# Attention, FFT mixing and FFN on one core: the FFN of batches 1 to 7 in one block of 512 tokens each and a last block of the left-over 448, with TensorE in program order there

## The chip, the cores and the metric

The program runs on one NeuronCore of a Trainium2 chip. A core has a matmul engine (TensorE, PE in the profile), VectorE (DVE), ScalarE (ACT), GpSimd (POOL) and SyncE (SP), which issues most DMAs here. The metric is the device time of one execution in microseconds; the median of three runs before the change is 1087.92 us (1087.62 to 1090.3).

## The reference

Eight batches of 576 tokens. The first half is attention over 8 heads with keys and values averaged over groups of 8 tokens; its result x (576 x 512 per batch) goes through a two-dimensional FFT of which the real part is kept, a residual, a normalization and a feed-forward network (FFN) of width 2048:

```python
attn = softmax(scale * q @ pool8(k).T) @ pool8(v)      # 8 x 8 heads x 576 x 64
x = attn, heads side by side                           # 8 x 576 x 512
X = np.fft.fft(np.fft.fft(x, axis=1), axis=2)
u = x + np.real(X)
mu = np.mean(u, axis=-1, keepdims=True)
var = np.mean((u - mu) ** 2, axis=-1, keepdims=True)
un = (u - mu) / np.sqrt(var + 1e-06)
ch = np.maximum(un @ w_ch1, 0.0) @ w_ch2
return u + ch
```

## The kernel before

Channels lie on the 128 partitions in four tiles (E0, O0, E1, O1), tokens along the free dimension. Each fp32 operand of the two large products is held as a high and a low part, so a product takes three matmul passes: high by high, high by low, low by high.

The **front end** of a batch, `fe(b)`, is a generator that works in steps: loads and averages keys and values, scores (psS, L345), softmax, transposition (psT, psR), attention times values (psX, L432, two halves of 288 tokens per group of heads), then the FFT as cosine and sine matmuls over sums of mirrored positions. The sum of the even channels is `tmpE` (L510), its parts are `f` (L503 on ScalarE, L504 on VectorE), and psA (L547), psB (L575), psQ and psP (L592) are the products. Then come the mean (psM, L638 to L643), the centred values in two parts `unh` and `unl`, the squares (`qh`, and `ql` L664), the variance (psVar, L667) and three Newton steps for the inverse root `rb`. All matmuls of the front ends use rotating PSUM banks that a function `bank` gives out.

The **FFN**, `ffn` (L705), works through the hidden width in 16 slices f of 128. For each f it issues 12 matmuls into g1 (L731), the relu `hh` on ScalarE (L735), its low part `hl` on VectorE (L736), and 12 matmuls into four accumulators acc0 to acc3 (L715) for the slice before. It yields after each such group of 12 matmuls; this is a half step. After the last slice VectorE multiplies the accumulators by `rb` (L745), adds U (L746), and SP sends the result out (L748). The low parts of the weights are kept in DRAM and read back for every f of every block, 256 KB for each of the two products (`load_low`, L214, in a ring of seven buffers with the tag "w"); the high parts stay on chip.

Unnormalized sums U, `unh`, `unl` and `rb` have a ring of two batches, 1152 columns. `blocks()` (L71) lists the blocks of the FFN: batch 0 in two halves of 288 tokens, each in two parts of 8 slices; batches 1 to 6 as nine blocks of 384 tokens over the ring, so a block may lie across two batches; batch 7 as two blocks of 288. That makes 208 slice steps.

The order of the instructions on each engine is fixed when the program is built, by a scheduler that plays the program through with its own durations: on TensorE it may take front-end matmuls and FFN matmuls in another order than the code has them. The code sets when a front-end step is issued: `advance(pos)` (L790) runs one step of each front end per half step, from positions in `free` (L753).

Of the kernel before, what the change touches and what calls it, by code (L numbers as in the profile page):

```python
# [83 lines left out]
def tile_kernel(ctx: ExitStack, tc: tile.TileContext, qt, kt, vm, vr, w1, w2, cad, cbd, mkd, out):  # L84
# [93 lines left out]
    def prep_w(n):  # L178
# [4 lines left out]
        if wide:  # L183
# [61 lines left out]


    def fe(b):
# [82 lines left out]
        def scores(gi, i):  # L330
# [374 lines left out]
    def ffn(ro, nb, to, f0, f1):  # L705
        cl = slice(ro, ro + nb)
        acc = [pp.tile([P, 512], F32, tag=f"acc{e}", name=f"acc{to}_{f0}_{e}")[:, 0:nb] for e in range(4)]
# [224 lines left out]
```

## Time and profile before

| | before |
|---|---|
| median of 3 runs | 1087.92 us |
| the profiled execution: time, span | 1088.63 us, 1086.9 us |
| TensorE busy | 1044.1 us, 96% |
| VectorE, ScalarE, GpSimd busy | 609.4, 415.0, 249.4 us |
| from the first matmul of 384 columns to the last matmul's start | 244.5 to 1080.1 us |

Busy time of an engine counts its computing instructions; a matmul is pipelined, so its listed duration is longer than the time by which the next one follows. The time from one matmul to the next is read from the starts in the timeline.

### The profile page before, as it was taken

To read this page: it belongs to the slowest core of one execution; us is meant where nothing else is said; L and a number is where in the kernel's file an instruction comes from. 1 tells how busy PE (TensorE), PEld (TensorE's weight loads), DVE (VectorE), ACT (ScalarE), POOL (GpSimd) and SP (SyncE) were. 2 spreads that over 40 slices of the span, in tenths; PEclk is the share of its full clock that TensorE was granted. 3 is DMA by queue.
4 is the path that set the end of the run, shared out by engine and by line. 5 is a ranking of instruction groups with operands and counts; after the bars stand their busy time and mean duration, and the time that the engine had idled before them with its cause. 6 is when DMAs were issued, how large, how long until landed. Compare 5 with 4: busy or idle time off the path is not lost.

```text
span 1086.9 us, 17702 instructions
## 1 busy us (share of the span) xinstructions
PE 1044.1 (96%) x6606; PEld 1018.9 (94%) x6606; DVE 609.4 (56%) x1237; ACT 415.0 (38%) x1102; POOL 249.4 (23%) x249
## 2 busy tenths in 40 slices
PE   8848898999999999999999999999999999999997
PEld 7737788999999999999999999999999999999997
DVE  7686878856376455756277455656467434522212
ACT  6767764543143341443233341443324422311110
POOL 4464355312240032201240122300331101300000
PEclk9878998999999999999999999999999999999999
DMA  7767976675445454445444454445435334446563
GB/s 246 259 215 249 330 253 213 191 201 165 127 122 162 123 167 133 128 141 162 139 122 147 140 155 132 135 125 156 158 108 157 97 107 123 115 131 185 166 187 99
DMA packets 91878, 175.80 MB, mean 162 GB/s; under 512 B 10128, under 2 KB 17296, under 8 KB 91536
## 3 DMA queue, kind: packets, MB, share of 16 engines
q1 hardware_dynamic: 91504, 172.01, 51.7%
q0 software_dynamic: 288, 2.66, 0.6%
q8 instruction: 52, 0.85, 0.3%
q14 instruction: 34, 0.28, 0.1%
HBM read 156.81 MB, written 17.83 MB: 161 GB/s over the span
## 4 chain that ended last, share of the span: by engine, by line
PE 85%; DVE 5%; DMA 4%; ACT 2%; POOL 2%; issue 1%; SPq 0%; DVEq 0%; POOLq 0%; ACTq 0%
PE acc L715 35%; PE g L731 35%; PE psX L432 3%; PE psS L345 3%; PE psP L592 2%; DMA k<-in_kt 1%; PE psA L547 1%; PE psB L575 1%; PE psT L385 1%; PE psQ L592 1%; DVE wd L199 1%; POOL k L280 1%; DMA w2l<-wd 1%; DVE wd L198 1%; PE psR L408 1%
## 5 line engine op out<-in xcount | busy, mean ns | idle before, releaser
L735 ACT ACTIVATE hh<-g 128x384 fp32r<-128x384 f32 (+1 forms) x208 | 96.2, 463 | 305.4 <-PE g L731 285.6
L736 DVE SCALAR_TENSOR_TENSOR hl<-g,hh 128x384 fp32r<-128x384 f32 (+1 forms) x208 | 108.6, 522 | 185.0 <-ACT hh L735 179.4
L715 PE MATMUL acc<-hh,w2h 128*128 128x384 f32 (+1 forms) x832 | 190.5, 329 | 0.2 <-DVE U L746 0.2
L715 PE MATMUL acc<-hh,w2low 128*128 128x384 f32 (+1 forms) x832 | 186.8, 327 | 0.3 <-DMA w2low<-w2l 0.3
L715 PE MATMUL acc<-hl,w2h 128*128 128x384 f32 (+1 forms) x832 | 182.3, 328 | 1.1 <-DVE hl L736 1.1
L731 PE MATMUL g<-unh,w1low 128*128 128x384 f32 (+1 forms) x832 | 178.2, 329 | 1.6 <-DMA w1low<-w1l 1.6
L731 PE MATMUL g<-unl,w1h 128*128 128x384 f32 (+1 forms) x832 | 177.8, 328 | 1.0 <-DVE unl L633 1.0
L731 PE MATMUL g<-unh,w1h 128*128 128x384 f32 (+1 forms) x832 | 175.6, 328 | 0.0
L715 PEld LDWEIGHTS acc<-hh,w2h 128*128 128x128 f32 x832 | 143.1, 189 | 2.6 <-ACT hh L735 0.7
L715 PEld LDWEIGHTS acc<-hh,w2low 128*128 128x128 f32 x832 | 144.0, 189 | 0.6 <-DMA w2low<-w2l 0.5
L715 PEld LDWEIGHTS acc<-hl,w2h 128*128 128x128 f32 x832 | 141.4, 190 | 2.1 <-DVE hl L736 1.7
L731 PEld LDWEIGHTS g<-unh,w1low 128*128 128x128 f32 x832 | 141.0, 190 | 2.0 <-DMA w1low<-w1l 1.8
L731 PEld LDWEIGHTS g<-unl,w1h 128*128 128x128 f32 x832 | 140.7, 190 | 1.4 <-DVE unl L633 1.3
L731 PEld LDWEIGHTS g<-unh,w1h 128*128 128x128 f32 x832 | 140.7, 191 | 1.3 <-issue 0.8
L364 POOL TENSOR_TENSOR t<-t,sm 128x720 f32<-128x720 f32 x32 | 47.0, 1469 | 284.6 <-DVE sm L363 247.3
L280 POOL TENSOR_TENSOR k<-k 128x288 f32<-128x288 f32 (+1 forms) x56 | 42.3, 755 | 97.1 <-DMA k<-in_kt 73.3
L624 POOL TENSOR_TENSOR U<-X,U 128x576 f32<-128x576 f32 (+1 forms) x14 | 20.0, 1433 | 124.9 <-DVE X L608 124.9
L345 PE MATMUL psS<-kpb,q 128*128 128x144 f32 x280 | 43.2, 289 | 3.8 <-DVE X L608 2.1
L345 PEld LDWEIGHTS psS<-kpb,q 128*128 128x128 f32 x280 | 39.8, 191 | 4.2 <-issue 2.3
L349 DVE TENSOR_REDUCE mx<-psS 128x6 f32<-128x432 f32 (+1 forms) x64 | 33.1, 525 | 18.9 <-PE psS L345 18.6
L360 ACT ACTIVATE t<-t 128x720 f32<-128x720 f32 x30 | 24.1, 804 | 37.3 <-DVE t L358 37.0
L745 DVE TENSOR_TENSOR acc<-acc,rb 128x384 f32<-128x384 f32 (+1 forms) x60 | 29.0, 518 | 13.8 <-PE acc L715 13.5
(209 smaller groups left out, 1425.7 us busy)
## 6 DMA issues: line engine op xcount, KB each, us to landing
w1low<-w1l SPq DMA_DIRECT2D x208, 256.0 KB, 2.7
w2low<-w2l SPq DMA_DIRECT2D x208, 256.0 KB, 2.9
wst<-in_w SPq DMA_DIRECT2D x30, 512.0 KB, 4.7
q<-in_qt SPq DMA_DIRECT2D x28, 288.0 KB, 3.1
k<-in_kt SPq DMA_DIRECT2D x28, 288.0 KB, 2.9
v<-in_vm SPq DMA_DIRECT2D x28, 256.0 KB, 3.0
out<-U SPq DMA_DIRECT2D x18, 384.0 KB, 3.5
w1l<-wd SPq DMA_DIRECT2D x16, 256.0 KB, 4.4
```

Of the source, the lines that this page charges most:

```text
L280: nc.gpsimd.tensor_tensor(out=out if n == 1 else src[:, :, 0:n], in0=src[:, :, 0] if n == 1 else src[:, :, 0:n], in1=src[:, :, 1] if n == ...
L345: mm = nc.tensor.matmul(ps[:, c * W2J:(c + 1) * W2J], lhsT=q[:, r0:r0 + P], rhs=kpb[g % 2], start=True, stop=True)
L349: nc.vector.tensor_reduce(out=mx[:, c0:c0 + n], in_=pv, op=ALU.max, axis=AX.X, negate=(b, g) in SM)
L360: nc.scalar.activation(t, t, AF.Exp, scale=1.0 / 64.0)
L364: ins = nc.gpsimd.tensor_tensor(out=t, in0=t, in1=sm.unsqueeze(3).broadcast_to([P, 5, 2, J]), op=ALU.mult)
L432: last = nc.tensor.matmul(ps, lhsT=w, rhs=a, start=(i == 0), stop=(i == len(mm) - 1))
L592: nc.tensor.matmul(ps, lhsT=w, rhs=a, start=(i == 0), stop=(i == 6))
L715: nc.tensor.matmul(acc[e], lhsT=w[:, e], rhs=h, start=(f == f0 and x == 0), stop=(f == f1 - 1 and x == 2))
L731: nc.tensor.matmul(ps, lhsT=w[:, c], rhs=x[:, ti, cl], start=(n == 0), stop=(n == 11))
L735: nc.scalar.activation(hh, ps, AF.Relu)
L736: nc.vector.scalar_tensor_tensor(out=hl, in0=ps, scalar=0.0, in1=raw(hh), op0=ALU.max, op1=ALU.subtract)
L745: nc.vector.tensor_tensor(out=acc[e], in0=acc[e], in1=rb[:, cl], op=ALU.mult)
```

## The change

Batch 0 keeps its four parts of 288 columns. Each batch from 1 to 7 has one block of its first 512 tokens. The last 64 tokens of each (U, `unh`, `unl`, `rb`) are written to DRAM by `keep_rest` when the batch's front end ends, four DMAs, and read back by `load_rest` in the block of batch 7 after its fifth half step, into the ring's free half; a last block of 448 columns computes these. There are 160 slice steps in place of 208. The program's host part puts the tokens back in order.

Within each block from batch 1 on, TensorE is under `manual_schedule`: its instructions keep the order in which the code issues them. Tables give the half step of a block after which each front-end step is issued: PRE (steps up to the FFT, for the batch two ahead) and POST (the steps from the FFT on, for the next batch); PRE1, POST1 and LATE are for the first two blocks. Front ends from batch 2 on follow a new generator, `steady`, which does the same matmuls, with 22 steps before and 10 behind; `tmpE` and `f` come at the end of its 22nd step. While batch 0's FFN runs, `early` issues steps of front end 2.

The "w" ring has six buffers in place of seven, `hh` and `hl` have 512 columns, the first two batches' diagonal `dg` has a tile and a PSUM bank of its own (before: X[:, 1] and psVar's bank), and from batch 2 on GpSimd does two of the four sums at a block's end.

```diff
+NB = 512
+FIRST = 64
+RM = S - NB
+PRE = [2, 4, 7, 8, 10, 12, 15, 16, 18, 18, 19, 20, 21, 22, 23, 24, 25, 26, 28, 29, 30, 31]
...
+POST = [4, 5, 6, 9, 10, 11, 14, 15, 16, 17]
...
-    r = [(slot(0) + h * HS, HS, h * HS, f, f + 8) for f in (0, 8) for h in range(2)]
-    for m in range(3):
-        r += [(i * 384, 384, S + m * RING + i * 384, 0, NFC) for i in range(3)]
-    return r + [(slot(7) + h * HS, HS, 7 * S + h * HS, 0, NFC) for h in range(2)]
+    r = [(0, slot(0) + h * HS, HS, h * HS, f, f + 8) for f in (0, 8) for h in range(2)]
+    r += [(b, slot(b), NB, S + (b - 1) * NB, 0, NFC) for b in range(1, B)]
+    return r + [(B, slot(0), (B - 1) * RM, S + (B - 1) * NB, 0, NFC)]
...
+    def keep_rest(b):
+        cl = slice(slot(b) + NB, slot(b) + S)
+        for t, r in zip((raw(unh), raw(unl), U), rests):
+            nc.sync.dma_start(r[:, :, b - 1], t[:, :, cl])
+        nc.sync.dma_start(rests[3][:, 0, b - 1], rb[:, cl])
...
-        lows[i, n] = t = wk.tile([P, DM], F32R, tag="w", bufs=7, name=f"w{i + 1}low")
+        lows[i, n] = t = wk.tile([P, DM], F32R, tag="w", bufs=6, name=f"w{i + 1}low")
...
-        dg = X[:, 1]
+        dg = wk.tile([P, S], F32, tag="k", name="dg")
...
+        ps = bank(b, f"psD{b}", True)
...
-            nc.vector.tensor_tensor(out=acc[e], in0=acc[e], in1=rb[:, cl], op=ALU.mult)
-            nc.vector.tensor_tensor(out=u, in0=u, in1=acc[e], op=ALU.add)
+            v = raw(gt(2 + e, "v"))[:, 0:nb] if e < 2 and b > 1 else acc[e]
+            nc.vector.tensor_tensor(out=v, in0=acc[e], in1=rb[:, cl], op=ALU.mult)
+            (nc.gpsimd if e < 2 and b > 1 else nc.vector).tensor_tensor(out=u, in0=u, in1=v, op=ALU.add)
...
+        advance(2, min(len(PRE1), n2 + (len(PRE) - n2) * (pos + 1) / FIRST))
...
     for blk in blocks():
-        for _ in ffn(*blk):
...
+        b = blk[0]
+        with tc.manual_schedule(engines={mybir.EngineType.PE}) if b else ExitStack():
+            for h, _ in enumerate(ffn(*blk)):
+                if b == 0:
+                    early()
+                    pos += 1
+                    continue
+                if b == B - 1 and h == 4:
+                    load_rest(slot(0))
+                if b in LATE:
+                    advance(b + 1, len(PRE1) + sum(x <= h for x in LATE[b]))
+                pre, post = (PRE1, POST1) if b == 1 else (PRE, POST)
+                advance(b + 1, len(PRE) + sum(x <= h for x in post) if h >= post[0] else 0)
+                advance(b + 2, sum(x <= h for x in pre))
```

**TensorE at the start of batch 3's psA.** Names: acc576 belongs to the block of batch 1, g1_1088 to that of batch 2 (acc960 and g1_960 to a block of 384 before); psA3_0 and psA3_1 are the two groups, f holds high and low part of `tmpE`. Before:

```order
L715 MATMUL acc960_0_2_4063<-hl_4434,w2h_69 128x384
L715 MATMUL acc960_0_3_4064<-hl_4434,w2h_69 128x384
L731 MATMUL g1_960_13_4486<-unh_83,w1h6_1993 128x384 x4
L731 MATMUL g1_960_13_4486<-unl_84,w1h6_1993 128x384 x2
L547 MATMUL psA3_0_3795<-ca_70,f_3759 128x258 x4
L547 MATMUL psA3_1_3805<-ca_70,f_3759 128x258 x4
L547 MATMUL psA3_0_3795<-ca_70,f_3760 128x258 x2
L547 MATMUL psA3_0_3795<-ca_70,xe_79 128x258
L547 MATMUL psA3_1_3805<-ca_70,f_3760 128x258 x2
L547 MATMUL psA3_1_3805<-ca_70,xe_79 128x258
```

After, from the last matmuls of block 1:

```order
L926 MATMUL acc576_0_3_2949<-hh_3927,w2h7_2288 128x512
L926 MATMUL acc576_0_3_2949<-hh_3927,w2low_3841 128x512
L926 MATMUL acc576_0_3_2949<-hl_3928,w2h7_2288 128x512
L942 MATMUL g1_1088_1_4045<-unh_87,w1low_4020 128x512
L358 MATMUL psA3_0_4067<-ca_74,f_3981 128x258 x4
L358 MATMUL psA3_0_4067<-ca_74,f_3982 128x258 x2
L358 MATMUL psA3_0_4067<-ca_74,xe_83 128x258
L358 MATMUL psA3_1_4077<-ca_74,f_3981 128x258 x4
L358 MATMUL psA3_1_4077<-ca_74,f_3982 128x258 x2
L358 MATMUL psA3_1_4077<-ca_74,xe_83 128x258
L926 MATMUL acc1088_0_0_4016<-hh_4037,w2h_73 128x512
```

Where psA's two groups stood side by side in the middle of an FFN block, with the matmuls on the high part of both ahead of those on the low part, each group now stands whole, one behind the other, at the change from one block to the next.

**VectorE between the last psX of batch 3 and the low part of tmpE.** Names: X is the attention's result, rb and U belong to block 1. Before:

```order
L445 TENSOR_TENSOR X_80<-psX3_1_3736,X_80 128x288
L510 TENSOR_TENSOR tmpE_3755<-X_80 128x2x287
L327 SCALAR_TENSOR_TENSOR rw1_78<-vt_4805,mk_72,rw1_78 32x1
L277 TENSOR_REDUCE vs_5111<-v4_0_4929 128x64
L277 TENSOR_REDUCE vt_5109<-vr4_1_4931 32x64
L504 TENSOR_TENSOR f_3760<-tmpE_3755,f_3759 128x580
```

After:

```order
L651 TENSOR_TENSOR X_84<-psX3_1_3964,X_84 128x288
L328 TENSOR_TENSOR tmpE_3971<-X_84 128x2x287
L957 TENSOR_TENSOR acc576_0_0_2946<-acc576_0_0_2946,rb_86 128x512
L520 SCALAR_TENSOR_TENSOR wlo_4441<-vs_4438,mk_76,wh_4440 128x1
L529 SCALAR_TENSOR_TENSOR rw1_82<-vt_4322,mk_76,rw1_82 32x63
L529 SCALAR_TENSOR_TENSOR rw1_82<-vt_4322,mk_76,rw1_82 32x1
L957 TENSOR_TENSOR acc576_0_1_2947<-acc576_0_1_2947,rb_86 128x512
L957 TENSOR_TENSOR acc576_0_2_2948<-acc576_0_2_2948,rb_86 128x512
L957 TENSOR_TENSOR acc576_0_3_2949<-acc576_0_3_2949,rb_86 128x512
L958 TENSOR_TENSOR U_85<-U_85,acc576_0_0_2946 128x512
L340 TENSOR_TENSOR f_3982<-tmpE_3971,f_3981 128x580
```

The four products with rb and a sum of block 1's end, 512 columns each, now stand between `tmpE` and its low part (L340, before L504).

## Rows read from the trace of the kernel before

**Rows 1.** The page's first two parts: TensorE's busy time with its share of the span and its instructions, then the busy tenths of TensorE and of VectorE in 40 slices of 27.2 us.

```profile
PE 1044.1 (96%) x6606; PEld 1018.9 (94%) x6606; DVE 609.4 (56%) x1237; ACT 415.0 (38%) x1102; POOL 249.4 (23%) x249
PE   8848898999999999999999999999999999999997
DVE  7686878856376455756277455656467434522212
```

**Rows 2.** Busy time of the engines by stretch: the stretch in us and its length, then for each engine the busy time with its instructions, the granted TensorE clock, the DMA share and GB/s.

```profile
150.00:200.00 50.00, 44.13 (x298) 41.35 (x297) 39.42 (x78) 26.73 (x64) 28.40 (x33) 0.93 0.72 226
200.00:250.00 50.00, 50.00 (x378) 49.54 (x377) 30.78 (x81) 21.28 (x60) 7.41 (x5) 1.00 0.62 183
250.00:600.00 350.00, 350.00 (x2150) 347.23 (x2149) 204.32 (x407) 123.82 (x331) 76.65 (x74) 1.00 0.47 142
600.00:960.00 360.00, 360.00 (x2202) 357.17 (x2201) 195.85 (x388) 123.86 (x324) 67.31 (x60) 1.00 0.44 131
```

**Rows 3.** What TensorE waited for: us in total, times, longest us. In the stretch from 246 us to the end this view has no line.

```profile
PE psVar L698 <- DVE X L695: 3.7, 1, 3.7
```

**Rows 4.** The timeline: start in us, duration in us (merged rows: from the first start to the last end), engine, line, operation, tiles. The first row is the first matmul with 384 columns. The rows at 963.85 and 972.24 begin groups of one place in the loop and lie 48 matmuls with 384 columns apart; those at 986.62 and 996.18 lie 72 matmuls with 288 columns apart; the matmul at 403.97 follows the four with 256 columns at 403.50.

```profile
244.47 0.87 PE L731 MATMUL g<-unh,w1h 128*128 128x384 f32 x4
...
403.50 0.63 PE L575 MATMUL psB<-ca,f 128*128 128x256 f32 x4
403.97 0.33 PE L731 MATMUL g<-unl,w1h 128*128 128x384 f32 x1
...
963.85 0.33 PE L731 MATMUL g<-unh,w1h 128*128 128x384 f32 x1
...
972.24 0.34 PE L731 MATMUL g<-unh,w1h 128*128 128x384 f32 x1
...
986.62 0.29 PE L731 MATMUL g<-unh,w1h 128*128 128x288 f32 x1
...
996.18 0.29 PE L731 MATMUL g<-unh,w1h 128*128 128x288 f32 x1
```

**Rows 5.** Groups of TensorE's instructions with shapes apart (busy us, mean ns). Each of the two widths has six such groups, three of L715 and three of L731, with one count.

```profile
L715 PE MATMUL acc<-hh,w2h 128*128 128x384 f32 x576 | 137.7, 340 | 0.0
L715 PE MATMUL acc<-hh,w2h 128*128 128x288 f32 x256 | 52.8, 304 | 0.2 <-DVE U L746 0.2
```

**Rows 6.** Groups of VectorE's instructions with shapes apart: the product with rb at the end of a block, at both widths.

```profile
L745 DVE TENSOR_TENSOR acc<-acc,rb 128x384 f32<-128x384 f32 x36 | 19.3, 557 | 11.6 <-PE acc L715 11.6
L745 DVE TENSOR_TENSOR acc<-acc,rb 128x288 f32<-128x288 f32 x24 | 9.8, 458 | 2.2 <-PE acc L715 1.9 <-ACT rb L699 0.3
```

**Rows 7.** The timeline from the last psX of batch 3 (L432) over the sum of mirrored positions (L510) and its high and low part (L503, L504) to the first psA of that batch (L547).

```profile
385.04 0.30 PE L432 MATMUL psX<-R,rw 96*128 96x288 f32 x1
387.54 1.05 DVE L510 TENSOR_TENSOR tmpE<-X 128x574 f32<-128x574 f32 x1
389.87 0.68 ACT L503 CAST f<-tmpE 128x580 fp32r<-128x580 f32 x1
390.58 0.76 DVE L504 TENSOR_TENSOR f<-tmpE,f 128x580 fp32r<-128x580 f32 x1 [0.39 <-ACT f L503]
392.38 0.87 PE L547 MATMUL psA<-ca,f 128*128 128x258 f32 x6
```

**Rows 8.** The timeline of batch 5's variance: the last matmul of psM, the low part of the squares (L664), the first weight load of psVar (L667).

```profile
559.83 0.30 PE L643 MATMUL psM<-s,avg 128*128 128x288 f32 x1
...
572.44 1.77 DVE L664 TENSOR_TENSOR ql<-X,qh 128x576 fp32r<-128x576 f32 x1 [0.41 <-ACT qh L663]
...
574.64 0.19 PEld L667 LDWEIGHTS psVar<-qh,avg 128*128 128x128 f32 x1
```

**Rows 9.** Busy time by stretch, columns as in group 2: a stretch in which TensorE waits, the one behind it, and a later one.

```profile
126.00:130.00 4.00, 0.38 (x4) 0.14 (x2) 3.90 (x8) 3.19 (x6) 2.51 (x2) 1.00 0.99 347
130.40:133.60 3.20, 3.20 (x14) 2.64 (x13) 2.93 (x8) 0.92 (x2) 1.17 (x1) 0.50 1.02 353
168.00:174.00 6.00, 6.00 (x47) 5.94 (x46) 3.34 (x8) 3.60 (x8) 2.19 (x3) 1.00 0.64 194
```

**Rows 10.** The timeline of batch 3: the transposition of the remainder rows (L408) and the end of R (L418); the last matmul of a pair's first position (L432) and the last sum on its bank (L445).

```profile
372.99 0.60 PE L408 MATMUL psR<-ident,rt 128*32 128x128 f32 x4
374.82 0.68 DVE L418 TENSOR_TENSOR R<-psR,R 32x512 fp32r<-32x512 f32 x1 [3.39 <-ACT R L417]
...
379.42 0.29 PE L432 MATMUL psX<-R,rw 96*128 96x288 f32 x1
380.88 0.45 DVE L445 TENSOR_TENSOR X<-psX,X 128x288 f32<-128x288 f32 x1
```

**Rows 11.** A DMA issue of the page's part 6 (KB each, median us from issue to landing), and what SP's queue waited for from 180 to 246 us (us in total, times, longest us).

```profile
w1low<-w1l SPq DMA_DIRECT2D x208, 256.0 KB, 2.7
...
SPq L214 <- PE g L731: 16.1, 9, 2.2
SPq L214 <- PE acc L715: 11.2, 9, 2.4
```

**Rows 12.** The timeline of the program's end: the last four matmuls, then the products with rb and the sums of the last block.

```profile
1080.06 0.69 PE L715 MATMUL acc<-hl,w2h 128*128 128x288 f32 x4
1080.38 1.56 DVE L745 TENSOR_TENSOR acc<-acc,rb 128x288 f32<-128x288 f32 x4 [1.86 <-PE acc L715]
1081.85 1.53 DVE L746 TENSOR_TENSOR U<-U,acc 128x288 f32<-128x288 f32 x4
```

More of the change, by code (lines that the diff above doesn't have):

```diff
@@ L92, in tile_kernel @@
     wls = [dp.tile([P, NFC, DM], F32, name=f"w{i + 1}l") for i in range(2)]
+    rests = [dp.tile([P, n, B - 1, RM], F32, name=f"rest{i}") for i, n in enumerate((4, 4, 4, 1))]
     whs = [cp.tile([P, 12, DM], F32R, name=f"w{i + 1}h") for i in range(2)]
@@ L244, in tile_kernel, with unpack @@
     keep_busy(BUSY["start"])
+    def keep_rest(b):
[3 more added lines that the diff above has]
+        nc.sync.dma_start(rests[3][:, 0, b - 1], rb[:, cl])
+    def unpack(ps, src, last, n, l0, m, mat):
+        mm = []
+        for i in range(2):
+            h, l = src[i][:, l0:l0 + m], src[i][:, n + l0:n + l0 + m]
+            mm += [(h, mat[:, 2 * i]), (l, mat[:, 2 * i]), (h, mat[:, 2 * i + 1])]
+        k = 98 if n == 258 else 96
+        mm.append((last[0:k, l0:l0 + m], mat[0:k, 4]))
+        for i, (w, a) in enumerate(mm):
+            nc.tensor.matmul(ps, lhsT=w, rhs=a, start=(i == 0), stop=(i == 6))
@@ L328, in prep_v, with scores @@
             st["w", g] = (wh, wl)
-        def scores(gi, i):
+        def scores(gi, i, then=None):
             g = GROUPS[gi][i]
@@ L373, in scores @@
             st["t", g] = t
+            if b > 1:
+                if then:
+                    then(gi, i)
+                return
             yield
@@ L456, in fetch @@
                     load_rem(0)
+        if b > 1:
+            yield from steady(b, st, Xb, Ub, load, load_v, load_rem, prep_k, prep_v, scores, transposes, values, halves)
+            return
         fetch(3, True)
@@ L703, in tile_kernel, with ffn @@
     at = [0]
-    def ffn(ro, nb, to, f0, f1):
+    def ffn(b, ro, nb, to, f0, f1):
         cl = slice(ro, ro + nb)
-        acc = [pp.tile([P, 512], F32, tag=f"acc{e}", name=f"acc{to}_{f0}_{e}")[:, 0:nb] for e in range(4)]
+        acc = [pp.tile([P, NB], F32, tag=f"acc{e}", name=f"acc{to}_{f0}_{e}")[:, 0:nb] for e in range(4)]
         def gemm2(f, hh, hl, wh, wl):
@@ L749, in ffn, with load_rest @@
         yield
-    free = {1: 0, 2: 64, 3: 128, 4: 160, 5: 224, 6: 256, 7: 320}
-    npre = 20
-    done_w = 0
+    def load_rest(ro):
+        cl = slice(ro, ro + (B - 1) * RM)
+        for t, r in zip((raw(unh), raw(unl), U), rests):
+            nc.sync.dma_start(t[:, :, cl], r.rearrange("p n b s -> p n (b s)"))
+        nc.sync.dma_start(rb[:, cl], rests[3].rearrange("p n b s -> p (n b s)"))
+    done_w = [0]
     fe0, fe1 = fe(0), fe(1)
@@ L780, in tile_kernel @@
             n2 += 1
+    keep_rest(1)
     while n2 < STEPS:
@@ L783, in tile_kernel, with advance @@
         n2 += 1
-    run = {2: [fe2, n2, 0, None]}
-    def start(b, pos):
-        if b < B:
-            run[b] = [fe(b), 0, pos, None]
-    def advance(pos):
-        for b in sorted(run):
-            r = run[b]
-            if r[3] is None:
-                upto = (pos + 1 - r[2]) * (npre / (free[b] - 1) if b == 2 else 1)
-            else:
-                upto = r[3] + pos - max(free[b], r[2]) + 1 if pos >= free[b] else 0
-            while r[1] < upto:
-                said = next(r[0], "end")
-                r[1] += 1
-                if said == "U":
-                    r[3] = r[1]
-                    r[2] = pos
-                    break
-                if said == "free":
-                    start(b + 1, pos)
-                if said == "end":
-                    del run[b]
-                    break
+    fes = {2: [fe2, n2]}
+    def advance(b, upto):
+        if not 1 < b < B:
+            return
+        r = fes.setdefault(b, [fe(b) if b > 2 else fe2, 0])
+        while r[1] < upto:
+            next(r[0])
+            r[1] += 1
     def need(pos):
```

204 lines of the change are left out of this document (187 added, 17 removed).

## The prediction, made before the changed kernel ran

> **What bounds the kernel now.** I read the page's busy times first: TensorE works 1044.1 of 1086.9 us, and its slices stand at 9 from the ninth on; VectorE falls to 2 tenths near the end [rows 1]. The table by stretch says where the other 43 us are: up to 200 us TensorE has gaps (44.1 of 50 us), from 200 on none, at granted clock 1.00 [rows 2]; what TensorE waited for is empty from 246 us on [rows 3]. So behind the first matmul with 384 columns, at 244.5 us, the time to the last matmul at 1080.1 [rows 4, 12] is a count of matmuls times the distance of their starts. VectorE is busy 0.58 of 250 to 600 us, DMA 0.47 [rows 2]: both have room on average, not at each place. The kernel gains only by fewer or denser matmuls, and loses by any wait that its order adds. Something on another engine counts only if TensorE stands behind it.
>
> **Widths.** Of 16 x 3 x 8 = 384 matmuls that a block issues, nine blocks of 384 columns and two of 288 become seven of 512 and one of 448: 11 x 384 = 4224 matmuls become 3072, 1152 fewer. The columns stay the same (9 x 384 + 2 x 288 = 4032 = 7 x 512 + 448). The counts agree: six groups of 576 with 384 columns, and six of 256 with 288, half of them batch 0's, which stays [rows 5]. What a matmul costs beyond its columns decides. The starts at 963.85 and 972.24 lie 48 matmuls apart: 174.8 ns each; 986.62 and 996.18 lie 72 apart: 132.8 ns; four with 256 columns take 403.97 - 403.50 = 0.47 us, 117.5 ns each [rows 4]. Through the first two of these goes a line with 0.4375 ns per column and 6.8 ns per matmul; with the third I take 6.6. By the line 1152 matmuls less save 7.6 us. The bounds: 256 and 384 columns alone cost 0.459 and 0.455 ns per column, all but proportional, which saves nothing; and what stands above one column per cycle at 2.4 GHz is 174.8 - 160.0 = 14.8 ns at 384 columns, and if that were the same at every width 1152 x 15 = 17.3 us would go. I take the line, as it lies on three widths, for -7.6 (0 to -17.3). It puts 512 columns at 231 ns and a half step of 12 at 2.77 us.
>
> Here the Trainium skill ("TensorE: Matmul & The Clock Gate", Back-to-back issue gap) has a rule: at the full clock one matmul follows another after N/2.4 + 2.5 ns. That makes 162.5 ns at 384 columns, and the trace shows 174.8 [rows 4], so the measurement decides and the sum doesn't use the rule. By it 1152 matmuls less would save 2.9 us, and the sum below would end near 1093.5.
>
> **The seam from block 1 to block 2.** Order is now kept on TensorE, so a late operand stops it; before, the trace shows no such stop [rows 3]. The tightest place is the start of batch 3's psA. Before, the last psX ends at 385.34, then `tmpE` takes 1.05 us from 387.54, its parts start at 389.87 and 390.58, and the low part ends at 391.34, 6.0 us after psX; the matmuls start at 392.38, with about 40 wide ones in between [rows 7]. After, the order shows 12 accumulator matmuls and one of g1 between psX and psA: 13 x 0.231 = 3.0 us, and the two psA groups need the low part after four of their own matmuls, some 0.48 us later. On VectorE four products with rb and one sum, 512 columns each, stand ahead of the low part. By the products at 288 and 384 columns (458 and 557 ns [rows 6]) one of 512 takes 0.69 us. The tail of the chain, 1.05 + 0.68 + 0.76 us with the sums of X ahead, needs 3.8 us with nothing between; five wide operations add 3.4, and hand-overs about 1: the low part ends 8.3 us behind psX. TensorE waits 8.3 - 3.0 - 0.5 = 4.8 us (bounds 4 to 7 by the fastest and the observed chain). After a wait of this kind the row from 126 to 130 us shows what follows: TensorE busy 0.38 of 4 us, then 14 matmuls in 3.2 us at clock 0.50, the lower level (1.2 GHz), where a later stretch has 47 in 6 us at 1.00 [rows 9]. 3.2 us would have held 25, so the low clock costs about 11 x 0.15 = 1.7 us. Together +6.5. Queued behind psA on TensorE is the whole next block, so nothing hides it. In blocks 3 to 6 the table puts psX and psA further apart, and I price nothing there.
>
> **The variance of batch 2.** From the end of psM to psVar the chain takes 14.1 us: 560.13 to 574.21, where `ql` ends, and the weight load comes at 574.64 [rows 8]. The table of block 1 leaves four half steps and the pieces between, 4 x 2.77 + 1.4 = 12.5 us: +1.6 us (0 if VectorE is freer than at 560 us; 3 if it is not). The steady blocks leave 15.2. By the order, psA of batch 2 has 22 matmuls of 512 columns and four of its own behind psX, 5.6 us, against 6.0 [rows 7]: +0.4.
>
> **Pieces in the steady blocks.** R is ready 375.50 - 373.59 = 1.9 us after psR, and the order leaves a half step, 2.8; a bank is free 381.33 - 379.71 = 1.6 us after psX, where 3.3 are left [rows 10]. Nothing, but with slacks of 0.9 to 1.7 us: the price when that cover goes is a rival.
>
> **DMA and the ring.** 48 pairs of low halves of 256 KB fall away, 25 MB at 2.7 us each to land [rows 11]; 3 MB are written and read back in small packets. From 250 us on the DMA share is 0.44 to 0.47 and TensorE waits for none of it [rows 2, 3], so all this costs nothing. load_rest has 27 half steps, over 70 us, before its block. On SP's queue the writes stand behind the batch's last Newton step; the next loads of low halves are queued behind them, and the ring of six holds three slices' pairs, 5.5 us each, as cover. With seven, SP waited for TensorE to free a slot, 16.1 + 11.2 us from 180 to 246 us [rows 11], so loads ran as far ahead as the ring allowed; a slot less is 0 in the sum, and up to +4 in the first 245 us.
>
> **The first 245 us.** Batch 0's blocks are the same, and the order almost; `dg` has its own tile and bank. TensorE waited once for the chain to psVar, 3.7 us [rows 3]. I take it to be the chain itself and not the bank: 0 (-5.4 to +4).
>
> **The end.** The sums end 2.6 us behind the last matmul (1080.75 to 1083.38 [rows 12]). With 448 columns each product and sum takes some 0.62 us (between the widths of [rows 6] and 0.69), but the first accumulators are finished up to 9 matmuls, 1.8 us, ahead of the last, so about as much is left behind it; the last output DMA is larger by half. 0 (-0.5 to +1).
>
> **Sum.** -7.6 + 6.5 + 1.6 + 0.4 = +0.9 us on the profiled 1088.63: 1089.5. The profiled execution is 0.7 above the median, so the time is 1088.8 us. 0.3%, 3.3 us, is about what a measurement of this kernel tells from no change; the forecast lies within it.
>
> **Rivals.**
> - The matmul's extra is constant (15 ns, the upper bound): -17.3 in place of -7.6 gives 1088.8 - 9.7 = 1079.1. For it: 288 and 384 differ by only 2 ns of extra; against it: they do differ, and 256 columns have 10.8. Chance 0.20.
> - The wait for psVar at 126 us goes, as `dg` no longer shares tile and bank: -3.7 and -1.7 of low clock: 1083.4. For it: the wait ends on L695, which writes `dg` [rows 3]; against it: ten short steps of VectorE stand before it in any case. Chance 0.15.
> - Widths give nothing (proportional): 1088.8 + 7.6 = 1096.4, slower. For it: 256 and 384 columns [rows 4]; against it: 288. Chance 0.13, with the case between it and the forecast. (The rule of the Trainium skill named above is such a case, at 1093.5.)
> - The kept order makes TensorE wait in each steady block too: at R and at a bank's release, where the slack is 0.9 and 1.7 us [rows 10], three wide operations of 0.69 us ahead of the chain, 2.1 us, would leave 1.2 us of wait at R, 0.4 at the bank and some 0.4 of low clock: 2 us in each of five blocks, +10: 1098.8, slower. It decides from chains 1 us longer than the trace's. For it: VectorE's share of 0.58 [rows 2], and the psA chain which took 6.0 us where 3.8 would do; against it: the wider blocks give each half step 2.77 us in place of 2.1. Chance 0.15.
> - TensorE's order is not what limits, or the first 245 us shift for another reason: no shape of its own. Chance 0.03.
> The forecast keeps 0.34.
>
> **How the numbers follow.** The forecast's own range is 1086 to 1092. The range of eight in ten goes from the constant extra at 1079 to the steady waits at 1099. Faster by over 0.3%: 0.20 + 0.15 = 0.35. Same: 0.34. Slower: 0.13 + 0.15 + 0.03 = 0.31.
>
> **What would show it.** Starts of 512-column matmuls 231 ns apart for the widths: 225 and less mean the constant extra, 234 none. A wait of TensorE for the low part of tmpE (L340) of 4 to 7 us between blocks 1 and 2, with a clock below 1.00 behind it, and one of about 1.6 us for ql at batch 2's psVar. No waits in blocks 3 to 6, the first 512-column matmul within 4 us of 244.5, no wait for load_rest. It is wrong if waits stand in the steady blocks, or if the start of block 1 moves.

## The result, and the profile after

The changed kernel takes 1095.97 us (median of 4 runs, 1094.71 to 1097.25) against 1087.77 us before: a ratio of 1.0074, 95% interval 1.005 to 1.0097. It is slower, by 8 us. The profiled execution has a span of 1094.6 us, 7.7 more than before. Two statements ahead of the prediction need correcting. In `steady`, `tmpE` and `f` come in the 18th step and psA in the 20th, not in the 22nd; the 22 steps reach to psB. And 1080.1 us is the start of the last four matmuls of the kernel before; the very last one starts at 1080.45.

TensorE is busy for 1041.1 us of the changed kernel's span, with 5454 matmuls. The busy times by stretch, columns as in [rows 2]:

```profile
250.00:300.00 50.00, 48.88 (x256) 41.20 (x256) 29.04 (x61) 15.55 (x47) 16.16 (x17) 1.00 0.44 139
300.00:350.00 50.00, 48.52 (x234) 40.19 (x233) 35.00 (x62) 24.40 (x59) 10.89 (x8) 0.97 0.31 92
350.00:400.00 50.00, 45.08 (x230) 37.08 (x230) 28.45 (x59) 16.10 (x50) 8.82 (x13) 0.93 0.42 136
400.00:900.00 500.00, 500.00 (x2507) 419.30 (x2506) 291.49 (x540) 180.25 (x454) 125.68 (x104) 1.00 0.36 112
```

From 400 us on TensorE has no gap. The gaps lie between 250 and 400 us, in block 1 and at its end, where the kernel before had none [rows 2]. What TensorE waited for behind 246 us (us in total, times, longest), where the view of before was empty [rows 3]:

```profile
PE psA L358 <- DVE f L340: 3.8, 2, 2.7
PE psA L358 <- ACT f L339: 1.9, 1, 1.9
PE psVar L436 <- DVE ql L431: 1.4, 1, 1.4
PE acc L926 <- DVE U L958: 0.3, 1, 0.3
```

All four lines belong to three places: psA of batch 2 (1.1 us), psVar of batch 2 (1.4 us), and the seam from block 1 to block 2 with psA of batch 3 (1.9 and 2.7 us, then 0.3 us for an accumulator). The timeline of the seam:

```profile
369.19 0.30 PE L638 MATMUL psX<-R,rw 96*128 96x288 f32 x1
...
371.02 1.36 DVE L328 TENSOR_TENSOR tmpE<-X 128x574 f32<-128x574 f32 x1
...
372.31 0.69 DVE L957 TENSOR_TENSOR acc<-acc,rb 128x512 f32<-128x512 f32 x1
...
373.14 1.49 DVE L529 SCALAR_TENSOR_TENSOR rw<-vt,mk,rw 32x63 fp32r<-32x63 f32 x2
374.36 0.83 PE L358 MATMUL psA<-ca,f 128*128 128x258 f32 x4 [1.89 <-ACT f L339]
374.56 1.88 DVE L957 TENSOR_TENSOR acc<-acc,rb 128x512 f32<-128x512 f32 x3
376.47 0.69 DVE L958 TENSOR_TENSOR U<-U,acc 128x512 f32<-128x512 f32 x1
377.07 0.79 DVE L340 TENSOR_TENSOR f<-tmpE,f 128x580 fp32r<-128x580 f32 x1
...
377.92 0.80 PE L358 MATMUL psA<-ca,f 128*128 128x258 f32 x2 [2.73 <-DVE f L340]
...
380.83 1.27 DVE L958 TENSOR_TENSOR U<-U,acc 128x512 f32<-128x512 f32 x2
381.55 1.10 PE L926 MATMUL acc<-hh,w2h 128*128 128x512 f32 x2 [0.27 <-DVE U L958]
```

The last psX ends at 369.49, the low part of `tmpE` at 377.86, 8.4 us later; four products with rb and a sum stand ahead of it. (The high part was late too, on ScalarE, behind two copies that waited for GpSimd; as psA needs the low part after four matmuls, the low part sets the sum of both waits.) The last two rows show what ends the seam: block 2's first matmuls into the accumulators, one for each of the four, need block 1's sums, and the fourth starts at 382.15, right behind VectorE's last sum, which ends at 382.10. Behind the low part, and behind the wait at psVar, the granted clock is at the lower of its two levels (1.2 GHz):

```profile
314.00:316.00 2.00, 0.59 (x2) 0.38 (x3) 2.00 (x2) 0.81 (x2) 1.13 (x1) 1.00 0.39 127
318.00:320.00 2.00, 2.00 (x6) 1.62 (x5) 1.52 (x2) 0.38 (x2) 0.00 (x0) 0.50 0.00 0
378.00:380.00 2.00, 2.00 (x9) 2.00 (x10) 2.00 (x4) 0.88 (x3) 0.03 (x1) 0.50 0.48 139
```

Two groups of four matmuls with 512 columns in this stretch start 1.71 us apart, 0.427 us for each:

```profile
317.55 1.91 PE L926 MATMUL acc<-hh,w2low 128*128 128x512 f32 x4
319.26 1.54 PE L926 MATMUL acc<-hl,w2h 128*128 128x512 f32 x4
```

The Trainium skill ("TensorE: Matmul & The Clock Gate", Wait — 56ns, not 53.3ns?) gives 426.7 ns for 512 columns at 1.2 GHz; the trace agrees.

The widths, in block 7 and the last block, where nothing but FFN matmuls runs. The two pairs of rows lie 168 matmuls apart:

```profile
884.93 0.40 PE L942 MATMUL g<-unh,w1h 128*128 128x512 f32 x1
...
923.78 0.39 PE L942 MATMUL g<-unh,w1h 128*128 128x512 f32 x1
...
1017.29 0.36 PE L942 MATMUL g<-unh,w1h 128*128 128x448 f32 x1
...
1051.49 0.36 PE L942 MATMUL g<-unh,w1h 128*128 128x448 f32 x1
```

That is 231.3 ns at 512 columns and 203.6 at 448, against 174.8 at 384 and 132.8 at 288 before [rows 4]. The FFN of batches 1 to 7 takes 2688 x 0.2313 + 384 x 0.2036 = 699.9 us in place of 3456 x 0.1748 + 768 x 0.1328 = 706.1: -6.2 us.

From here on three stretches of one profile are compared: the "early part" from the first psM (65.14 before, 63.02 after) to the first matmul with 384 or 512 columns, the "main part" from there to the last matmul's start, and what lies around them.

| | before | after | difference |
|---|---|---|---|
| start of the first psM | 65.1 | 63.0 | -2.1 |
| early part | 179.3 | 182.4 | +3.1 |
| main part | 836.0 | 842.5 | +6.5 |
| rest of the span | 6.4 | 6.6 | +0.2 |

In the main part the three places cost, against the pitch of their matmuls, 1.4 us (266.7 to 271.1), 3.6 us (313.6 to 324.1) and 7.6 us (372.1 to 386.2): 12.6 us, of which the view of waits has 7.4. 12.6 - 6.2 = 6.4, which is the 6.5 us but for rounding. The rest of the 12.6 is not all the price of the low clock. At the seam psA's last ten matmuls ran at clock 0.50; at full speed they would have ended some 1 us earlier, and TensorE would have stood until the same last sum at 382.10.

### The profile page after: what moved, and what is told of

The parts are those of the page before. It is cut to its first block, busy times and chain, and to the rows that moved or that the text cites. A ratio compares the mean times of both kernels' runs of the same rounds, so it can differ in the third digit from the quotient of the medians.

```text
span 1094.6 us, 15096 instructions
## 1 busy us (share of the span) xinstructions
PE 1041.1 (95%) x5454; PEld 889.0 (81%) x5454; DVE 601.7 (55%) x1151; ACT 408.7 (37%) x1054; POOL 272.5 (25%) x263
## 4 chain that ended last, share of the span: by engine, by line
PE 80%; DVE 10%; DMA 4%; ACT 3%; issue 1%; POOL 1%; SPq 0%; DVEq 0%; POOLq 0%; ACTq 0%
PE g L942 34%; PE acc L926 33%; PE psX L638 3%; PE psS L547 2%; DMA wst<-in_w 2%; PE psP L270 1%; PE psA L358 1%; PE psT L591 1%; PE psB L371 1%; PE psQ L270 1%; DVE wd L208 1%; DMA w2l<-wd 1%; DVE wd L207 1%; PE psR L614 1%; DVE mx L551 1%
## 5 line engine op out<-in xcount | busy, mean ns | idle before, releaser
L947 DVE SCALAR_TENSOR_TENSOR hl<-g,hh 128x512 fp32r<-128x512 f32 (+2 forms) x160 | 101.5, 634 | 260.2 <-ACT hh L946 259.4
L946 ACT ACTIVATE hh<-g 128x512 fp32r<-128x512 f32 (+2 forms) x160 | 88.6, 554 | 355.2 <-PE g L942 354.9
L926 PE MATMUL acc<-hh,w2h 128*128 128x512 f32 (+2 forms) x640 | 171.3, 378 | 4.0 <-ACT hh L946 3.1
L926 PE MATMUL acc<-hl,w2h 128*128 128x512 f32 (+2 forms) x640 | 166.5, 375 | 7.3 <-DVE hl L947 7.3
L926 PE MATMUL acc<-hh,w2low 128*128 128x512 f32 (+2 forms) x640 | 167.3, 373 | 0.0
L942 PE MATMUL g<-unh,w1h 128*128 128x512 f32 (+2 forms) x640 | 166.5, 380 | 0.0
L942 PE MATMUL g<-unl,w1h 128*128 128x512 f32 (+2 forms) x640 | 163.6, 376 | 1.3 <-DVE unl L843 1.3
L942 PE MATMUL g<-unh,w1low 128*128 128x512 f32 (+2 forms) x640 | 161.6, 373 | 0.7 <-DMA w1low<-w1l 0.6
L926 PEld LDWEIGHTS acc<-hh,w2low 128*128 128x128 f32 x640 | 116.9, 190 | 19.5
L926 PEld LDWEIGHTS acc<-hh,w2h 128*128 128x128 f32 x640 | 113.0, 190 | 22.7 <-ACT hh L946 4.4
L547 PE MATMUL psS<-kpb,q 128*128 128x144 f32 x280 | 40.1, 288 | 1.4 <-ACT w2h L212 1.4
L547 PEld LDWEIGHTS psS<-kpb,q 128*128 128x128 f32 x280 | 38.3, 191 | 3.5 <-ACT w2h L212 1.6
```

Of the source, the lines that this page charges most:

```text
L547: mm = nc.tensor.matmul(ps[:, c * W2J:(c + 1) * W2J], lhsT=q[:, r0:r0 + P], rhs=kpb[g % 2], start=True, stop=True)
L926: nc.tensor.matmul(acc[e], lhsT=w[:, e], rhs=h, start=(f == f0 and x == 0), stop=(f == f1 - 1 and x == 2))
L942: nc.tensor.matmul(ps, lhsT=w[:, c], rhs=x[:, ti, cl], start=(n == 0), stop=(n == 11))
L946: nc.scalar.activation(hh, ps, AF.Relu)
L947: nc.vector.scalar_tensor_tensor(out=hl, in0=ps, scalar=0.0, in1=raw(hh), op0=ALU.max, op1=ALU.subtract)
```

## The experiments

Each is compared by its median and by the two parts of its one profile. In the three profiles with the old order (before, e8, e10) the main part is 836.0 to 836.6 us and the early part 177.4 to 179.6; the times of the kernel before range from 1085 to 1091 us.

| run | median us | ratio to before (95%) | early | main |
|---|---|---|---|---|
| changed kernel | 1095.97 | 1.0074 (1.005 to 1.0097) | 182.4 | 842.5 |
| e1_var_later | 1095.11 | 1.0062 (1.0039 to 1.0085) | 181.6 | 838.7 |
| e2_seam_and_var | 1096.97 | 1.0078 (1.0056 to 1.0101) | 182.9 | 841.5 |
| e3_no_order_first | 1114.55 | 1.0243 (1.0213 to 1.0272) | 182.2 | 860.4 |
| e4_fill_wait | 1098.55 | 1.0099 (1.0069 to 1.0129) | 181.9 | 844.8 |
| e5_el_gpsimd | 1097.69 | 1.0094 (1.0067 to 1.0122) | 183.6 | 842.3 |
| e6_psx_earlier | 1090.08 | 1.0027 (1.0013 to 1.004) | 183.6 | 835.3 |
| e7_fill_short | 1094.83 | 1.0074 (1.0059 to 1.0089) | 183.1 | 840.0 |
| e8_dg_alone | 1085.58 | 0.9978 (0.9969 to 0.9988) | 177.4 | 836.6 |
| e9_newton_later | 1087.23 | 0.9998 (0.9988 to 1.0008) | 180.5 | 832.5 |
| e10_ring_six | 1087.47 | 0.9998 (0.9988 to 1.0007) | 179.6 | 836.1 |
| e11_tables_mended | 1090.11 | 1.0018 (1.0005 to 1.0031) | 178.9 | 834.0 |
| e12_old_front_end_2 | 1090.02 | 1.0016 (1.0006 to 1.0026) | 182.3 | 836.1 |

What the places in blocks 1 and 2 cost in each profile, against the pitch of their matmuls as above (us; a star where the clock fell to 0.50 behind the wait):

| run | psA of batch 2 | psVar of batch 2 | psS in block 1, for R | seam |
|---|---|---|---|---|
| changed kernel | 1.4 | 3.6* | 0 | 7.6* |
| e1 | 0 | 0 | 2.0 | 7.0* |
| e2 | 0 | 0 | 6.7* | 5.1* |
| e4 | 1.4 | 3.6* | 0 | 9.9 |
| e5 | 1.4 | 2.1 | 0 | 8.8* |
| e6 | 0 | 0 | 2.0 | 3.6* |
| e7 | 1.4 | 2.1 | 0 | 6.1 |
| e9 | 0 | 0 | 0 | 2.2 |
| e11 | 0 | 0 | 1.9 | 2.2 |

Without them the main part is 829.7 to 830.4 us in each of these. Two things in this table are not the work of any edit. The wait at psVar is 1.4 us in the changed kernel, e4, e5 and e7 alike, but the clock fell behind it only in the first two, which makes 1.5 us. And the seam lasts until VectorE's last sum: but for e4 the fourth accumulator's first matmul starts 0.05 to 0.06 us behind it in each. So two main parts that lie less than some 3 us apart are told apart only place by place.

**Later places for batch 2 (e1).**

```diff
-LATE = {1: [5, 6, 7], 2: [1, 2, 3]}
+LATE = {1: [6, 7, 8], 2: [1, 2, 3]}
-POST1 = [9, 10, 11, 13, 14, 15, 17, 18, 19, 20]
+POST1 = [9, 10, 11, 13, 14, 15, 18, 19, 20, 21]
```

> Batch 2's psA, psB and its variance are issued one half step later in block 1 (2.77 us more room each); all else as changed. Theory A (the loss is waits at three fixed places and the low clock behind them): the wait for ql (1.4 us by the waits, 1.7 in the starts) and the one for f before batch 2's psA (1.3 us) go, and with them about 1.9 us of low clock behind the first: -4.5 to -5 us, about 1091. Theory B (block 1 is short of VectorE as a whole): the waits only move to other tiles of block 1 and the time stays at 1095 to 1097.

The waits for ql and for batch 2's f are gone; a new one of 1.5 us for R stands in block 1, the seam's remain:

```profile
PE psA L358 <- ACT f L339: 2.1, 1, 2.1
PE psS L547 <- DVE R L624: 1.5, 1, 1.5
PE psA L358 <- DVE f L340: 1.0, 1, 1.0
```

The main part falls by 3.8 us; the medians (-0.9 us) don't tell the two apart, and 1095.1 lies in theory B's range. Theory A is right that the waits at these places and the low clock behind psVar go, but a piece put later meets the next one on VectorE, as theory B said of the waits.

**The seam too (e2).** PRE1 with its last steps earlier, LATE[2] and POST one half step later for block 2 (core of the edit, on top of e1; the 3rd to 5th of batch 4's steps in block 2 come a half step later too):

```diff
-PRE1 = [2, 6, 12, 12, 15, 16, 19, 20, 21, 21, 23, 24, 25, 25, 27, 28, 29, 30, 30]
+PRE1 = [2, 6, 12, 12, 15, 16, 19, 20, 20, 21, 22, 23, 24, 24, 26, 27, 28, 29, 30]
...
+LATE = {1: [6, 7, 8], 2: [2, 3, 4]}
+POST2 = [5, 6, 7, 9, 10, 11, 14, 15, 16, 17]
```

> As the run before, and batch 3's psA one half step later in block 2, its psX one half step earlier in block 1. Theory A: all of the 7.4 us of waits behind 246 us and the 4 to 5 us of low clock go: -11 to -12 us, 1084 to 1085, faster than the kernel before. Theory B: 1092 or more, with new waits for VectorE between 250 and 400 us.

A miss for theory A; the time and the new waits are theory B's. No wait at psA or psVar is left, yet 6.0 us stand elsewhere:

```profile
PE psS L549 <- DVE R L626: 3.3, 2, 2.0
PE acc L928 <- ACT hh L948: 2.0, 1, 2.0
PE acc L928 <- DVE U L960: 0.7, 1, 0.7
```

With psA out of the way the next block's first accumulation comes sooner, and waits for its `hh` and for the accumulators that VectorE has still to read. With steps 8 and 9 both at half step 20, the next psS stands close behind R and waits for it. So at the seam TensorE waits for whichever late result the order puts next, of VectorE or, as with `hh`, of ScalarE.

**TensorE free in blocks 1 and 2 (e3).**

```diff
-        with tc.manual_schedule(engines={mybir.EngineType.PE}) if b else ExitStack():
+        with tc.manual_schedule(engines={mybir.EngineType.PE}) if b > 2 else ExitStack():
```

> TensorE free to reorder in the blocks of batches 1 and 2, in program order from batch 3 on; tables as changed. Theory A (it is the kept order that turns late operands into waits): the waits at psA of batches 2 and 3 and at batch 2's psVar go, 1084 to 1087. Theory B (the operands are late whatever the order): waits of 5 us or more remain, 1092 and more.

The busy times by stretch:

```profile
246.00:400.00 154.00, 154.00 (x768) 128.68 (x768) 86.04 (x171) 54.01 (x148) 27.43 (x28) 1.00 0.39 121
400.00:500.00 100.00, 89.61 (x433) 73.37 (x432) 59.99 (x115) 38.12 (x97) 24.97 (x24) 0.91 0.33 98
500.00:600.00 100.00, 93.96 (x470) 78.98 (x469) 62.00 (x117) 38.85 (x101) 28.63 (x27) 0.92 0.35 106
```

Two of its waits behind 246 us:

```profile
PE psA L358 <- ACT f L339: 4.4, 1, 4.4
PE psX L638 <- DVE t L560: 2.1, 2, 1.6
```

In the two free blocks TensorE never stops, as before the change. But the scheduler fills them with FFN work and leaves front-end work behind: the first two blocks hold 317 front-end matmuls where the changed kernel has 417, the third 284 where it has 184. This first block with kept order, which begins at 465 us, then meets the work late, with the clock low for most of 474 to 515 us, and the whole is 18 us slower. The time is in theory B's range, but neither theory had this: a free block ahead of ordered ones hands them its backlog.

**The clock (e4, e7).** Small matmuls on the identity ahead of batch 3's psA, 44 and 18 of them:

```diff
+            if b == 3 and i == 0:
+                for _ in range(18):
+                    nc.tensor.matmul(ps[:, 0:P], lhsT=ident, rhs=ident, start=True, stop=True)
```

> 44 small matmuls on the identity stand before batch 3's psA, into the bank that psA then overwrites; they fill the wait of 5 us and change nothing else. If the clock falls because TensorE stands still there, the granted clock stays at 1.00 behind the seam and the time falls by 2 to 2.5 us, to about 1093.7. If the clock falls for another reason (VectorE's load, say), the time stays or rises by as much as the small matmuls outlast the wait, 1096 to 1097.

> As the run with 44 small matmuls, with 18, which last 4.0 us at 0.22 us each and so end inside the wait. If standing still lowers the clock: clock 1.00 behind the seam and the main phase about 2 us shorter, 840.5 us. If not: 842.5 us.

The 44 took 9.7 us (0.22 us each, twice what I had reckoned) and outlasted the wait: main part +2.3 us, but with clock 1.00 through the seam. The 18 ended just as the low part of `tmpE` came, so that psA ran without a wait:

```profile
372.00:377.00 5.00, 5.00 (x46) 5.00 (x45) 4.97 (x10) 2.23 (x5) 3.24 (x5) 1.00 0.49 164
377.00:384.00 7.00, 5.79 (x30) 4.25 (x29) 3.64 (x8) 2.25 (x7) 1.55 (x3) 1.00 0.68 212
```

VectorE is as full as without them (4.97 of 5 us, against 4.94 in the changed kernel) and the clock stays at 1.00, in both runs; without them it fell at this seam in all three profiles with the same tables or e1's (changed kernel, e5, e1). So it is TensorE's standing still and not VectorE's load that lowers it. Standing still isn't enough, though: behind the same wait at psVar the clock stayed at 1.00 in e7:

```profile
316.39 0.40 PE L439 MATMUL psVar<-ql,avg 128*128 128x288 f32 x1 [1.41 <-DVE ql L434]
...
316.00:322.00 6.00, 5.61 (x26) 4.64 (x27) 4.40 (x8) 1.38 (x3) 0.00 (x0) 1.00 0.22 76
```

The main part is 2.5 us shorter, about as expected, but not by the clock at the seam: 1.5 us of it are the low clock that didn't come at psVar, and 1.5 us are a shorter chain on VectorE, on which two operations ahead of the low part took 1.36 us in place of the 2.85 (L328, and L529, here L532) in the changed kernel:

```profile
370.04 0.75 DVE L328 TENSOR_TENSOR tmpE<-X 128x574 f32<-128x574 f32 x1
...
371.55 0.61 DVE L532 SCALAR_TENSOR_TENSOR rw<-vt,mk,rw 32x63 fp32r<-32x63 f32 x2
```

(0.5 us more than before stand at a single matmul at 597 us.) The medians lie 1.1 us apart, within their spread.

**The low part of tmpE on GpSimd (e5).**

```diff
-        nc.vector.tensor_tensor(out=el, in0=tmp, in1=raw(eh), op=ALU.subtract)
+        (nc.gpsimd if b == 3 else nc.vector).tensor_tensor(out=el, in0=tmp, in1=raw(eh), op=ALU.subtract)
```

> In batch 3 alone GpSimd and not VectorE subtracts for the low part of tmpE (L340). Theory A (five wide operations of block 1's end stand ahead of it on VectorE): the low part comes about 1.5 us behind the high one, the wait for f L340 falls from 2.7 to under 1.2 us, the main phase is about 2 us shorter than the 842.5 us of the changed kernel. Rival (the sum of mirrored positions is late itself, and all VectorE work at the seam): the high part's wait stays and the time moves to acc or psB: within 1 us of 842.5.

```profile
375.77 0.75 PE L358 MATMUL psA<-ca,f 128*128 128x258 f32 x4 [1.62 <-ACT f L339]
375.79 1.33 POOL L340 TENSOR_TENSOR f<-tmpE,f 128x580 fp32r<-128x580 f32 x1
...
377.18 0.50 PE L358 MATMUL psA<-ca,f 128*128 128x258 f32 x2 [0.67 <-POOL f L340]
...
379.72 0.49 PE L926 MATMUL acc<-hh,w2h 128*128 128x512 f32 x1 [1.08 <-DVE U L958]
...
382.08 0.49 PE L926 MATMUL acc<-hh,w2h 128*128 128x512 f32 x1 [1.87 <-DVE U L958]
...
383.35 1.39 PE L926 MATMUL acc<-hh,w2h 128*128 128x512 f32 x2 [0.77 <-DVE U L958]
```

The low part's wait falls from 2.73 to 0.67 us, as theory A said, and 1.08 + 1.87 + 0.77 us come back a few matmuls later, at accumulators that VectorE hasn't read. The main part is unchanged, as the rival said, though only because no low clock followed the wait at psVar in this execution: the seam itself takes 8.8 us and not 7.6. The products ahead of `f` made it late, but they are due at nearly the same time themselves.

**The whole chain earlier (e6, e9, e11).** With the 11th to the 18th of batch 3's steps in block 1 a half step earlier (eight steps, not seven), the last psX stands 37 matmuls with 512 columns ahead of psA, and `tmpE` with both parts is done before block 1's products begin (on top of e1; e9 and e11 move Newton steps as well):

```diff
-PRE1 = [2, 6, 12, 12, 15, 16, 19, 20, 21, 21, 23, 24, 25, 25, 27, 28, 29, 30, 30]
+PRE1 = [2, 6, 12, 12, 15, 16, 19, 20, 21, 21, 22, 23, 24, 24, 26, 27, 28, 29, 30]
...
+POST1 = [9, 10, 11, 13, 14, 15, 18, 19, 22, 23]    # e9
+POST1 = [9, 10, 11, 13, 14, 15, 18, 19, 22, 22]    # e11
```

> Tables of the first run (batch 2's psA and variance a half step later), and batch 3's last seven steps in block 1 one half step earlier, so that its last psX stands 36 and not 13 matmuls ahead of psA and the low part of tmpE comes ahead of block 1's products on VectorE. Theory A (places in the order): all waits behind 246 us below 1 us together and the clock at 1.00: 842.5 - 7.4 - 4.3 = about 831 us from the first 512-column matmul to the last, 1084 to 1085. Rival (VectorE is full at this seam): waits of 4 us or more at other tiles between 320 and 400 us, 1091 or more.

> The tables of the run with psX earlier, and batch 2's last two Newton steps three half steps later, away from the place where batch 3's R waits behind them on VectorE. Theory A (places in the order): the wait of 1.5 us for R goes; what stays is the accumulator's bank at the seam (0.7 us and its low clock): main phase 833 to 834 us against 835.3, 1088 us. Rival (VectorE is full in block 1): the wait only moves, 835 to 836 us, 1090 us.

> The changed kernel with the mended tables: batch 2's psA and variance a half step later, batch 3's last steps of block 1 a half step earlier, batch 2's last two Newton steps at half step 22, ahead of batch 3's first values. (In the run with Newton steps at 22 and 23 the last one of batch 2 reads a tile that batch 3 has begun to overwrite, so that batch's root is another; the work is the same.) Theory A: main phase 832 to 834 us, first wide matmul at 245 to 248, 1086 to 1088 us, within 0.3% of the kernel before. Rival: two Newton steps side by side hold VectorE and a wait of 1 us or more returns, 1089 or more.

What is left of the waits in e6 (in e9 only the accumulator's 0.7 us and 0.4 us for `hh`):

```profile
PE psS L547 <- DVE R L624: 1.5, 1, 1.5
PE acc L926 <- DVE U L958: 0.7, 1, 0.7
PE acc L926 <- ACT hh L946: 0.2, 1, 0.2
```

e6 takes 7.2 us off the main part (11.5 were expected): between its theory and its rival. e9 takes 10.0, to 832.5, under the 836.0 of the kernel before and half a us under the expected 833 to 834; but e9 is no replacement: it lacks batch 2's right root, for the reason given in e11's expectation. e11's waits are e6's within 0.1 us: the wait for R is back, as the rival said. Its main part is 834.0 all the same, as no low clock followed at the seam, where e6 had one (2.2 us lost there against 3.6). The times are 1090.1, 1087.2 and 1090.1 us. e11's profiled execution took 1084.2 us, its others 1086.5 to 1092.0; as only one is profiled, where these lost their time isn't shown.

**dg alone (e8), a ring of six (e10), the old generator for batch 2 (e12).**

```diff
-        dg = X[:, 1]
+        dg = wk.tile([P, S], F32, tag="k", name="dg")     # e8
...
+        ps = bank(b, f"psD{b}", True)                     # e8
...
-tag="w", bufs=7
+tag="w", bufs=6                                           # e10
...
-        if b > 1:
+        if b > 2:                                         # e12, on e11
             yield from steady(b, st, Xb, Ub, load, load_v, load_rem, prep_k, prep_v, scores, transposes, values, halves)
```

> The kernel before with the first two batches' dg in a tile and a bank of its own, nothing else. If the wait of 3.7 us for psVar came from the shared tile or bank, it goes with its low clock and the time falls by 5 us, to about 1083. If it came from VectorE's chain, which is busy 9.8 of 10 us there, another wait takes its place and the time stays within 2 us of the kernel before.

> The kernel before with six buffers in the ring of weight pieces in place of seven, nothing else. If the smaller ring is what lengthens the changed kernel's first 245 us (by 1 us in its profile, by about 2 over the profiles of all runs with its early order): the first matmul of 384 columns comes 1 to 3 us after 244.5 and the time is 1088.5 to 1090.5. If not: within 1 us of the kernel before.

> As the run with mended tables, but batch 2's front end is the generator of the kernel before, placed at the same half steps. From the first psM to the first wide matmul the kernels with the changed order take 180.5 to 183.6 us in their profiles, those with the old one 177.4 to 179.6. If the new generator's order of batch 2 is what costs these 3 us: 177 to 180 us, and 1083 to 1085 us in all. If not (the wide tiles, the drift of weight loads): 181 us or more and 1086 to 1088 us, or more where a wait appears in block 1.

In e8 the wait that rival 2 would have removed is still there, now on psD:

```profile
PE psD L699 <- DVE dg L695: 4.2, 1, 4.2
```

So neither tile nor bank was its cause. The kernel is nevertheless 0.2% faster than before, interval clear of 1, and the only one tried that beats both; why it gains isn't settled. In the kernel before the smaller ring changes nothing. With batch 2's old generator the early part is 182.3 us, not the 177 to 180 that its theory asked for: one profile against the new generator as the cause. (Its main part is 2.2 us longer than e11's: a new wait at psB of batch 2, and the low clock at the seam.)

## Why the prediction was wrong in its likeliest case, and right in most of its steps

The forecast was 1088.8 us, no change; the time came out 7.2 us above it, slower, inside the range of eight in ten but outside the forecast's own 1086 to 1092. That the range held is luck as to the cause: its upper part stood for widths that save nothing (1096.4) and for waits in the steady blocks (1098.8), and neither came. The steps in turn:

- Bound by the count and pitch of TensorE's matmuls from the first wide one on: right. Outside the three places TensorE never stops there.
- Widths: -7.6 forecast, -6.2 by the rows, 5.4 ns per matmul in place of 6.6. The constant extra (first rival) and none at all (third) both fall: 512 columns take 231.3 ns, not 234, nor the 228 that a constant extra of 15 ns gives (the 225 in the prediction is a slip). Above one column per cycle at 2.4 GHz the extra is 12.8 ns at 288 columns and 18.0 at 512.
- Seam: the wait came as worked out (low part 8.3 us behind psX forecast, 8.4 measured; 4.8 us of wait forecast, 1.9 + 2.7 measured). 6.5 forecast, 7.6 lost. The 1.7 us for the low clock behind the wait (1.4 by the pitch in [rows 9], 6 us for 47 matmuls) stand in the sum for something else: the clock did fall, for psA's last ten matmuls and about three into the accumulators, but TensorE had to wait for block 1's last sum on VectorE in any case. The forecast counted the sum ahead of the low part and not the three behind it, which the next block needs; that the term came near is luck.
- Variance of batch 2: 1.6 forecast, 3.6 lost. The wait itself was 1.4 and cost 2.1 by the starts (e5, e7); **the step that failed is that I priced no low clock behind it**, having priced one at the seam. It came in this profile and in e4, 1.5 us, and not in e5 and e7; why is open. psA of batch 2: 0.4 forecast, 1.4 lost.
- Steady blocks and DMA: 0 forecast, 0 measured; load_rest is waited for by nobody. The fourth rival falls.
- The first 245 us: 0 forecast. The psVar wait went, but not through the tile (e8): waits of batch 0's FFN for `hl` and `hh` took its place, with VectorE busy 9 of 10 us around 125 us before and after. The early part is 177.4 to 179.6 us in three profiles with the old order and 178.9 to 183.6 in eleven with the changed one, about 3 us more on average. In the result's own pair 2.1 us of it are hidden by an earlier start. The traces show where the time goes: from 100 to 241 us TensorE waits 9.9 to 11.2 us in the three profiles and 11.5 to 15.4 in the eleven, 2.7 more on average, and of this 1.1 to 2.8 us in the three and 6.7 to 11.2 in the eleven are for `hl` and `hh`. In the changed kernel's profile:

```profile
PE acc L926 <- DVE hl L947: 7.3, 4, 2.7
PE acc L926 <- ACT hh L946: 3.1, 4, 1.3
```

  Why these come later there stays open: e10 speaks against the ring, in the kernel before, and e12 against the generator, and no run took away the steps of front end 2 that `early` issues in this stretch.

The errors are 1.4 (widths), 1.1, 2.0 and 1.0 (the three places) and 1.2 (start, early part and end together): 6.7 of the 6.8 us between the forecast span and the measured one, all of one sign. The waits at the three places end on what VectorE owes (`ql`, `f`, U) but for the high part of `f`, and were summed as if independent. What stays unexplained of the e-runs is why a mended main part (832.5 to 834) doesn't show fully in the medians; the early part is the likely place, and it wasn't profiled often enough to tell.

## What to carry to other kernels

A kept order on the bounding engine can cost twice for a late operand: the wait, and the low clock behind it, which came behind some waits and not behind others of the same length. Count both at every place, but find first which late result ends the wait: behind it a low clock costs, ahead of it next to nothing. Start with the blocks in which two pipelines meet. A place is mended by moving the whole chain that feeds it; moving one link, or its engine, brings the wait back at the next operand that is owed (e2, e5). Wider tiles saved only some 5 ns for each matmul that went, so a change made for them has little to spend on waits.

## What the runs showed of the hardware that was not expected

- The clock did not fall behind each wait: the 1.4 us at psVar were followed by clock 0.50 in the changed kernel and in e4, by 1.00 in e5 and e7. The row from 266 to 270 us, with 1.1 us of waiting, is at 1.00 too, and so is all of 328 to 340 us in e6, with 1.5.

```profile
266.00:270.00 4.00, 2.88 (x20) 2.50 (x19) 3.91 (x7) 1.74 (x4) 2.29 (x3) 1.00 0.55 176
```

- Some of VectorE's operations are much longer while GpSimd works: at the seam L529 took 1.49 us for two instructions (1.36 and 0.20) that take 0.20 to 0.28 us each where GpSimd rests, and L328 1.36 us, while GpSimd ran two operations in the same time; the same sum takes 0.74 us where GpSimd rests (before the change, at 260 us) and took 1.05 in [rows 7], where GpSimd worked too. Not every operation beside GpSimd is longer: L328 took 0.74 us in e6, where it began 0.08 us ahead of GpSimd's next operation. The Trainium skill ("SBUF — State Buffer", SBUF: two separate sides) says that a VectorE instruction with two inputs from SBUF and a GpSimd one that reads SBUF exclude each other on a shared port for a whole instruction; these rows agree, and no run took GpSimd's work away to prove it:

```profile
370.97 1.70 POOL L482 TENSOR_TENSOR k<-k 128x288 f32<-128x288 f32 x2 [5.30 <-DMA k<-in_kt]
...
373.02 1.40 POOL L342 TENSOR_TENSOR tmpO<-X 128x576 f32<-128x576 f32 x1
```
